# Attention in bursts of three on borrowed MLP banks: 49 bursts in place of 73 in a fused attention and MLP kernel

## Chip, cores, metric

One core of a Trainium2 chip. The metric is the time of one execution on the device in microseconds (us).

## The reference

```python
# q, k, v: (8, 12, 448, 64);  w_in: (768, 2048);  w_out: (2048, 768);  alpha: (2048,)
scores = matmul(q, k.T) / sqrt(64)
attn_out = matmul(maximum(scores, 0) ** 2 / 448, v)
x = attn_out.transpose(0, 2, 1, 3).reshape(3584, 768)
h = x @ w_in
out = (maximum(h, 0) + alpha * minimum(h, 0)) @ w_out
```

## The kernel before

The engines are named as in the profile: PE is the tensor engine (PEld its weight loads), ACT is ScalarE, DVE is VectorE, POOL is GpSimd, SP issues DMAs. Matmul results go to PSUM, of which the kernel uses eight banks (two pairs and four); a bank gets its next tile only when ACT or DVE have read the last one.

The heads of a batch are taken four at a time: a "quad", three per batch, 24 in all. A quad has seven chunks of scores, each 4 matmuls on 64*64 quarters of the array, then A@V, 28 such matmuls. Each batch has an MLP in two stages: "in" (16 tiles `hps` of 6 matmuls, 128*128) and "out" (tiles `ops` of 16 matmuls in two half steps; 12 half steps in even batches, 16 in odd ones). The attention of batch b+1 is put in bursts between the MLP steps of batch b.

```python
sc_ps = pool("scps", 2, **PSUM)      # two pairs of banks: a chunk of scores, or an A@V
mm_ps = pool("mmps", 4, **PSUM)      # four banks for hps and ops
neg_pool = pool("neg", 3)

def scores(n, j, relu="act", space=sc_ps):
    ...                                          # 4 matmuls into two banks
    if relu == "both":                           # one bank by ACT, one by DVE
        nc.scalar.activation(rl[:, 0], half[0][:, :S], ACTF.Relu)
        nc.vector.tensor_scalar(rl[:, 1], half[1][:, :S], 0.0, None, ALU.max)
    ...
    else:
        nc.scalar.activation(rl, ps[:, :, :S], ACTF.Relu)

def squares(...):  nc.vector.tensor_tensor(a, rl, rl, ALU.mult)      # for each chunk

def ffn1(b, ff, ...):                            # one hps tile
    ...                                          # 6 matmuls
    nc.scalar.activation(neg, ps, ACTF.Relu, scale=-1.0)
    nc.vector.scalar_tensor_tensor(gT[...], neg, beta_sb[...], ps, ALU.mult, ALU.add)

def burst(n, i):                                 # four per quad
    if i == 0:                                   # chunk 0, then A@V of the quad before
        scores(n, 0); squares(); attnv(n - 1)
    else:                                        # chunks 2i-1 and 2i
        for j in (2 * i - 1, 2 * i):
            scores(n, j, ...); squares()
    if i == 0: load(n + 2)                       # each cut here: n below the number of quads
    if i == 1: transpose(n + 1, "k"); transpose(n + 1, "q")     # by DMA
    if i == 2: to_bf16(n + 2, w, nc.gpsimd)      # casts of k, q, v on GpSimd

for b in range(2, B - 1):                        # 12 bursts over the 28 or 32 steps of a batch
    spread(steps(b, "in") + steps(b, "out"), work[12 * b - 11:12 * b + 1])
```

## Time and profile before

| | before |
|---|---|
| time, median of the first 3 runs | 405.86 us (405.38 to 406.36) |
| span in the profile | 403.4 us |
| tensor engine (PE) busy | 390.4 us, 97% |
| attention bursts in the stream of quads 6 to 23 | 73 |

PE is busy nearly always, so the question is what it is busy with. The prediction shows the chain and a stretch of PE's timeline. Three groups of the page: line, engine, operation, output<-input, shapes and count; then total busy us and mean ns of one; then the engine's idle time before them.

```profile
L170 ACT ACTIVATE rl<-sc 128x896 bf16<-128x896 f32 x156 | 136.2, 919 | 80.0 <-PE sc L159 76.7
L181 DVE TENSOR_TENSOR at<-rl 128x896 bf16<-128x896 bf16 x167 | 115.2, 702 | 55.2 <-ACT rl L170 51.0
L236 DVE SCALAR_TENSOR_TENSOR gT<-neg,beta_sb,hps 128x448 bf16<-128x448 f32 x128 | 84.8, 676 | 31.8 <-ACT neg L235 30.7
```

Every chunk costs one ReLU on ACT and one square on DVE; every hps tile ends in one gT update on DVE, and only then is its bank free. Both engines mostly wait for someone else, and neither bounds the kernel.

### The profile page before, as it was taken

To read this page: it belongs to the slowest core of one execution; us is meant where nothing else is said; L and a number is where in the kernel's file an instruction comes from. 1 tells how busy PE (TensorE), PEld (TensorE's weight loads), DVE (VectorE), ACT (ScalarE), POOL (GpSimd) and SP (SyncE) were. 2 spreads that over 40 slices of the span, in tenths; PEclk is the share of its full clock that TensorE was granted. 3 is DMA by queue.
4 is the path that set the end of the run, shared out by engine and by line. 5 is a ranking of instruction groups with operands and counts; after the bars stand their busy time and mean duration, and the time that the engine had idled before them with its cause. 6 is when DMAs were issued, how large, how long until landed. Compare 5 with 4: busy or idle time off the path is not lost.

```text
span 403.4 us, 7848 instructions
## 1 busy us (share of the span) xinstructions
PE 390.4 (97%) x3201; PEld 196.0 (49%) x3201; DVE 241.8 (60%) x379; ACT 232.1 (58%) x330; POOL 76.1 (19%) x88
## 2 busy tenths in 40 slices
PE   7689999999999999999999999999999999999995
PEld 4334455444555445544555445544455444555562
DVE  3966766687464793488643975556834666525411
ACT  5866745787564885387643876557653577524200
POOL 6653000033033330035000350033300300000000
PEclk9999999999999999999999999999999999999999
DMA  6999996593278941586065862379054720130033
GB/s 143 196 209 204 204 249 205 121 283 78 65 197 240 288 87 45 160 248 183 0 118 178 225 186 46 85 223 312 4 79 105 205 46 2 41 78 2 1 80 78
DMA packets 64164, 55.44 MB, mean 137 GB/s; under 512 B 35696, under 2 KB 59776, under 8 KB 64128
## 3 DMA queue, kind: packets, MB, share of 16 engines
q1 hardware_dynamic: 53152, 44.98, 41.6%
q0 software_dynamic: 10976, 9.96, 15.5%
q8 instruction: 25, 0.41, 0.4%
q14 instruction: 11, 0.09, 0.1%
HBM read 45.62 MB, written 11.01 MB: 140 GB/s over the span
## 4 chain that ended last, share of the span: by engine, by line
PE 90%; DMA 8%; issue 0%; ACT 0%; DVE 0%; SPq 0%; POOL 0%; POOLq 0%
PE ops L244 37%; PE hps L228 35%; PE sc L159 10%; PE av L199 7%; DMA qe<-in_q_dram 3%; DMA w_in_sb<-in_moe_w_in_dram 2%; DMA vb<-in_v_dram 2%; DMA kraw<-in_k_dram 1%; PE tps L134 1%; ACT xT L214 0%; DVE osb L252 0%; ACT ke L335 0%; SPq L321 0%; POOL ke L103 0%; PE warm L317 0%
## 5 line engine op out<-in xcount | busy, mean ns | idle before, releaser
L170 ACT ACTIVATE rl<-sc 128x896 bf16<-128x896 f32 x156 | 136.2, 919 | 80.0 <-PE sc L159 76.7
L228 PE MATMUL hps<-xT,w_in_sb 128*128 128x448 bf16 x768 | 154.8, 353 | 1.3 <-ACT xT L208 0.5
L244 PE MATMUL ops<-w_out_sb,gT 128*128 128x384 bf16 x896 | 154.3, 327 | 0.0
L181 DVE TENSOR_TENSOR at<-rl 128x896 bf16<-128x896 bf16 x167 | 115.2, 702 | 55.2 <-ACT rl L170 51.0
L244 PEld LDWEIGHTS <-gT 128*128 128x128 bf16 x896 | 84.0, 98 | 67.0 <-issue 14.5
L228 PEld LDWEIGHTS <-w_in_sb 128*128 128x128 bf16 x768 | 71.3, 98 | 79.0 <-issue 18.2
L236 DVE SCALAR_TENSOR_TENSOR gT<-neg,beta_sb,hps 128x448 bf16<-128x448 f32 x128 | 84.8, 676 | 31.8 <-ACT neg L235 30.7
L235 ACT ACTIVATE neg<-hps 128x448 f32<-128x448 f32 x128 | 69.8, 549 | 46.0 <-PE hps L228 45.4
L252 DVE COPY osb<-ops 128x384 f32<-128x384 f32 x56 | 31.1, 555 | 58.4 <-PE ops L244 58.4
L109 POOL CAST kb<-kraw 128x896 bf16<-128x896 f32 x16 | 16.1, 1007 | 210.4 <-DMA vraw<-in_v_dram 121.8
L159 PE MATMUL sc<-qT,kT 64*64 64x448 bf16 x652 | 50.8, 364 | 3.7 <-ACT rl L170 1.6
L199 PE MATMUL av<-at,vb 64*64 64x448 bf16 x616 | 33.1, 350 | 0.0
L159 PEld LDWEIGHTS <-kT 64*64 64x64 bf16 x672 | 14.5, 104 | 37.2 <-issue 33.7
L214 ACT ACTIVATE xT<-av 128x896 bf16<-128x896 f32 x21 | 19.3, 917 | 11.3 <-PE av L199 11.3
L199 PEld LDWEIGHTS <-vb 64*64 64x64 bf16 x672 | 19.7, 107 | 11.5 <-issue 1.7
L109 POOL CAST qb<-qraw 128x896 bf16<-128x896 f32 x16 | 20.0, 1250 | 0.0
L109 POOL CAST vb<-vraw 128x896 bf16<-128x896 f32 x16 | 18.6, 1165 | 0.4 <-DMA vraw<-in_v_dram 0.3
L144 POOL DMA_DIRECT2D w_in_sb<-in_moe_w_in_dram x12 | 7.5, 636 | 4.7 <-DMA vb<-in_v_dram 1.8
L168 DVE TENSOR_SCALAR rl<-sc 128x896 bf16<-128x896 f32 x6 | 6.5, 1086 | 2.9 <-PE sc L159 2.9
L317 PE MATMUL warm<-warm_x,warm_w 128*128 128x256 bf16 x24 | 4.6, 359 | 1.1 <-DVE warm_x L311 1.1
L134 PE MATMUL tps<-ident,ke 128*64 128x128 bf16 x84 | 3.7, 222 | 1.2 <-ACT rl L165 0.6
L107 ACT COPY kT<-tps 128x896 bf16<-128x896 bf16 (+1 forms) x4 | 3.2, 798 | 2.8 <-PE tps L134 2.7
(46 smaller groups left out, 59.0 us busy)
## 6 DMA issues: line engine op xcount, KB each, us to landing
out_dram<-osb SPq DMA_DIRECT2D x56, 192.0 KB, 2.7
qraw<-in_q_dram SPq DMA_DIRECT2D x19, 448.0 KB, 4.1
kraw<-in_k_dram SPq DMA_DIRECT2D x19, 448.0 KB, 5.0
vraw<-in_v_dram SPq DMA_DIRECT2D x18, 448.0 KB, 5.7
w_out_sb<-in_moe_w_out_dram POOLq DMA_DIRECT2D x2, 1536.0 KB, 20.2
w_in_sb<-in_moe_w_in_dram POOLq DMA_DIRECT2D x8, 192.0 KB, 8.4
w_in_sb<-in_moe_w_in_dram POOLq DMA_DIRECT2D x4, 384.0 KB, 9.9
vb<-in_v_dram POOLq DMA_DIRECT2D x6, 224.0 KB, 9.8
```

The costliest lines, as they stand in the source:

```text
L109: eng.tensor_copy(o, i)
L134: nc.tensor.transpose(ps[64 * s:64 * s + 64, j], t[:, s, j], ident)
L159: nc.tensor.matmul(half[r][64 * c:64 * c + 64, :S], kT[n][64 * r:64 * r + 64, j, c, :], qT[n][64 * r:64 * r + 64, :, c, :], start=True, st ...
L170: nc.scalar.activation(rl, ps[:, :, :S], ACTF.Relu)
L181: nc.vector.tensor_tensor(a, rl, rl, ALU.mult)
L199: nc.tensor.matmul(half[r][64 * s:64 * s + 64, :S], vb[n][64 * r:64 * r + 64, s, j, :], a[64 * r:64 * r + 64, s], start=(j == 0), stop=(j ...
L214: nc.scalar.activation(xT[b][:, g], ps[:, :, :S], ACTF.Copy, scale=out_scale)
L228: nc.tensor.matmul(ps, w_in_sb[:, km // 2, km % 2, bass.ts(ff, 128)], xT[b][:, km // 2, km % 2, :], start=(km == 0), stop=(km == KM - 1))
L235: nc.scalar.activation(neg, ps, ACTF.Relu, scale=-1.0)
L236: nc.vector.scalar_tensor_tensor(gT[b // 2][:, ff, (b % 2) * S:(b % 2) * S + S], neg, beta_sb[:, ff:ff + 1], ps, ALU.mult, ALU.add)
L244: nc.tensor.matmul(ps, gT[sb][:, ff, bass.ts(c, 128)], w_out_sb[:, ff, bass.ts(hf, 384)], start=(ff == 0), stop=(ff == KF - 1))
L252: nc.vector.tensor_copy(o[:, bass.ts(hf, 384)], ps)
```

## The change

Its intent: fewer bursts. Three units (a unit is a chunk or an A@V) go in one burst. There are only two pairs of score banks, so the first chunk of a burst borrows two of the four MLP banks. In the "in" stage ACT takes both its halves, in the "out" stage ACT and DVE one each. Most bursts go to the "out" stage. The DMA transposes move to the burst that holds chunk 0, and the A@V of a quad comes one chunk later.

```diff
+        elif relu == "act2":
+            for r in range(2):
+                nc.scalar.activation(rl[:, r], half[r][:, :S], ACTF.Relu)
...
-    for b in range(2, B - 1):
-        spread(steps(b, "in") + steps(b, "out"), work[12 * b - 11:12 * b + 1])
+    stream = []
+    for n in range(2 * NG, NQ):
+        for j in range(NJ):
+            stream.append((n, j))
+            if j == 1 and n > 2 * NG:
+                stream.append((n - 1, "av"))
+    stream.append((NQ - 1, "av"))
...      # parts: the first of 2 units, then of 3
+            units_ = sorted(units, key=lambda u: u[1] == "av")
+            for i, (n, j) in enumerate(units_):
+                if j == "av":
+                    attnv(n)
+                elif i == 0 and len(units_) == 3:
+                    scores(n, j, "act2" if phase == "in" else "both", mm_ps)
+                else:
+                    scores(n, j)
+            squares()
...      # chunk 0: load(n + 2), transpose(n + 1); chunk 4: to_bf16(n + 2)
+    for b in range(1, B - 1):
+        n_in, n_out = ((2, 6) if b % 2 else (3, 5))
...
+        spread(mlp[3:] if b == 1 else mlp, [group(x, "in") for x in parts[count:count + n_in]], 0.95)
+        spread(steps(b, "out"), [group(x, "out") for x in parts[count:count + n_out]], 0.92)
```

More of the change, by code (lines that the diff above doesn't have):

```diff
@@ L281, in burst @@
                 squares()
-        if n < n_pe:
-            return
-        if i == 0 and n + 2 < NQ:
-            load(n + 2)
-        if i == 1 and n + 1 < NQ:
-            transpose(n + 1, "k")
-            transpose(n + 1, "q")
-        if i == 2 and n + 2 < NQ:
-            for w in "kqv":
-                to_bf16(n + 2, w, nc.gpsimd)
     def spread(seq, bursts, share=0.92):
@@ L412, with group, f @@
         ffn1(1, ff, range(4, KM))
-    work = [(n, i) for n in range(2 * NG, NQ) for i in range(4)] + [(NQ, 0)]
-    mlp = steps(1, "in")
-    spread(mlp[3:] + steps(1, "out"), work[:13])
-    for b in range(2, B - 1):
-        spread(steps(b, "in") + steps(b, "out"), work[12 * b - 11:12 * b + 1])
+    stream = []
[5 more added lines that the diff above has]
+    stream.append((NQ - 1, "av"))
+    parts, todo_u = [], list(stream)
+    while todo_u:
+        m = 2 if not parts else 3
+        parts.append(todo_u[:m])
+        del todo_u[:m]
+    def group(units, phase):
+        def f():
+            units_ = sorted(units, key=lambda u: u[1] == "av")
[7 more added lines that the diff above has]
+            squares()
+            for n, j in units_:
+                if j == 0:
+                    if n + 2 < NQ:
+                        load(n + 2)
+                    if n + 1 < NQ:
+                        transpose(n + 1, "k")
+                        transpose(n + 1, "q")
+                if j == 4 and n + 2 < NQ:
+                    for w in "kqv":
+                        to_bf16(n + 2, w, nc.gpsimd)
+        return f
+    count = 0
+    for b in range(1, B - 1):
+        n_in, n_out = ((2, 6) if b % 2 else (3, 5))
+        if b == 1:
+            n_in += 1
+        if b == B - 2:
+            n_out = len(parts) - count - n_in
+        mlp = steps(b, "in")
+        spread(mlp[3:] if b == 1 else mlp, [group(x, "in") for x in parts[count:count + n_in]], 0.95)
+        count += n_in
+        spread(steps(b, "out"), [group(x, "out") for x in parts[count:count + n_out]], 0.92)
+        count += n_out
     for _, fn in steps(B - 1, "in") + steps(B - 1, "out"):
```

## The prediction

> **What bounds the kernel now.** I read the page first: the shares of the engines, then the chain that ended last, then the waits from 127 to 355 us (batches 2 to 6 of the stream that the change rewrites), then the timeline of the tensor engine at a burst.
>
> ```profile
> PE 390.4 (97%) x3201; PEld 196.0 (49%) x3201; DVE 241.8 (60%) x379; ACT 232.1 (58%) x330; POOL 76.1 (19%) x88
> PE 90%; DMA 8%; issue 0%; ACT 0%; DVE 0%; SPq 0%; POOL 0%; POOLq 0%
> ```
>
> PE is busy for 97% of the span and makes up 90% of the chain; the 8% of DMA is the start, before 35 us, which the change doesn't touch. In the view of the waits from 127 to 355 us no row has PE as the one that waits: everybody waits for PE. So only PE time counts, and the question is which PE time isn't arithmetic. The timeline of PE (start, duration, count last) shows it:
>
> ```profile
> 175.10 0.57 PE L159 MATMUL sc<-qT,kT 64*64 64x448 bf16 x8
> 175.60 3.58 PE L228 MATMUL hps<-xT,w_in_sb 128*128 128x448 bf16 x18
> 179.11 0.57 PE L159 MATMUL sc<-qT,kT 64*64 64x448 bf16 x8
> 179.62 2.44 PE L228 MATMUL hps<-xT,w_in_sb 128*128 128x448 bf16 x12
> 181.99 0.38 PE L159 MATMUL sc<-qT,kT 64*64 64x448 bf16 x4
> 182.20 1.49 PE L199 MATMUL av<-at,vb 64*64 64x448 bf16 x28
> ```
>
> Starts are measured; ends are modelled, so I use starts only. Record by record, hps matmuls start 189 ns apart and ops matmuls 163. Four 64*64 matmuls start within about 10 ns of each other and the next four some 190 later, so a quartet is one step of 189 ns. Take the time from the last MLP matmul before a burst to the second after it, less two MLP steps: 609 ns for 8 scores, 1744 for 4 scores and 28 av, 1554 for the 28 av alone. Less 2, 8 and 7 steps of 189 that is 231, 232 and 231 ns. So **every burst pays a fixed 0.231 us**, whatever its length, beside hps and ops alike (94 ns entering, about 24 inside the first quartet, 92 leaving, the rest in the first MLP steps).
>
> A second, smaller loss, in the timeline of all engines:
>
> ```profile
> 253.16 0.57 PE L159 MATMUL sc<-qT,kT 64*64 64x448 bf16 x8
> 253.60 1.73 ACT L170 ACTIVATE rl<-sc 128x896 bf16<-128x896 f32 x2 [1.48 <-PE sc L159]
> 253.67 1.47 PE L244 MATMUL ops<-w_out_sb,gT 128*128 128x384 bf16 x8
> 255.07 0.69 PE L159 MATMUL sc<-qT,kT 64*64 64x448 bf16 x8
> ```
>
> Where only half an ops tile (8 matmuls) lies between two bursts, the second quartet starts late, because the ReLU at 253.60 holds the second score bank pair until 255.33: 722 ns instead of 608, four times in the stream.
>
> **What the Trainium skill says.** "TensorEngine Tiling (Array Packing)", Key Properties: changing the tiling mode drains the tensor engine; the 94 and 92 ns at each end of a burst agree, and the trace adds the size of it. "TensorE: Matmul & The Clock Gate", Back-to-back issue gap: N/2.4 + 2.5 ns for an isolated warm matmul, so 189 for 448 columns and 162.5 for 384, and less (131 for 512) in a sustained stream. The trace has 189 and 163 in its streams: the first formula holds here, and MLP steps have nothing left to give. "SBUF — State Buffer", Who interferes with whom: a VectorE instruction with two SBUF inputs contends with a GpSimd one that reads SBUF. The trace agrees: squares (L181) take 0.625 us, and up to 1.37 us where a POOL cast runs. "PSUM — Partial Sum Buffer" says in its rules to evacuate promptly; the ReLU wait above is such a case.
>
> **The change part by part.**
>
> *Removed.* Before: 18 quads in four bursts plus a last one, 73 bursts (I counted 73 runs of 64*64 matmuls after 79 us). After: 18 x 7 chunks and 18 A@V are 144 units; a first burst of 2, 47 of 3, a last of 1 make 49. 24 fewer, 24 x 0.231 = 5.54 us, all on PE and so on the chain. The matmuls stay the same in number and size.
>
> *Removed, by spacing.* In the second MLP stage ("out") bursts now lie at least two ops half-steps (2.6 us) apart: before steps 0, 3, 5, 8, 10, 13 of 16 for odd batches, 0, 3, 5, 7, 9 of 12 for even ones. The four waits of 0.114 go: 0.46 us.
>
> *Added, "out" stage.* Three chunks at once: the first on two MLP banks, half by ACT (0.55 us, as L235), half by DVE (616 by L166), two on the score banks. From the burst's first score matmul, in us: the quartets end at 0.37, 0.56, 0.75; ACT begins 0.06 later, back to back about 0.44 for a half and 0.81 for a whole, so the ReLUs end near 0.98, 1.8, 2.6; the squares follow 0.03 later each, the third ends at 3.26. The next burst comes at 0.69 + 16 x 0.163 + 0.09 = 3.4 at the earliest. Its score banks have been free since 2.6, and the borrowed MLP banks since 1.05. A whole odd "out" stage gives DVE 15 squares, 6 halves and 8 copies (0.555), 17.5 us, in about 29 us of PE. Nothing new on the path.
>
> *Added, "in" stage.* Both halves go to ACT, before the whole chunks, so ReLUs end near 3.1 and the first gT update (DVE, 0.68) comes at 3.8 to 4.4 behind three squares. The fifth hps tile after the burst, first to need a bank that the MLP gives back, starts at 0.69 + 4 x 1.13 = 5.2. Slack 0.8 us without casts. Casts (k, q, v: 1.0, 1.25, 1.17 us) fall into this stage, as now (POOL is busy there and idle in the "out" stretches I looked at), and can lengthen two or three squares by 0.7 each. There are 15 such bursts; if one in four loses the slack and some 0.15 to 0.2 us more, that is about 0.6 us. This is the softest figure.
>
> *Moved.* The load of quad n+2 and the DMA transposes of n+1 go to the burst with chunk 0. Transposes land in 2.6 to 6.7 us and are needed a whole quad later, at the closest 11 us (even "out" stage); loads take 4 to 5.5. Hidden. A@V of a batch's last quad stands with three steps (3.9 us) left, and its eviction to xT takes 0.92, ending about 2.9 after the burst's start, when the MLP still has some 2.9 to do. Hidden. The at tiles at most meet a wait of DVE on the A@V of the same burst.
>
> Sum: 405.86 - 5.54 - 0.46 + 0.6 = 400.5 us.
>
> **The rivals.**
>
> *A wait for MLP banks in the "out" stage.* The ops tile under way at a burst is copied only behind the burst's three squares, from 3.2 to 3.75. If the four MLP buffers went in strict rotation, the next burst at 3.4 would get just that bank and wait 0.4 us. It happens where a burst of three score chunks in mid-tile is followed two steps later by one that borrows banks: twice in batches 2 and 4, once each in 1, 3, 5 and 6, 8 x 0.4 = 3.2 us, giving 403.1 to 403.7. Against it: the compiled kernel before doesn't take these four banks in rotation where borrowed and MLP tiles mix early on; it takes the one freed first, and here the two ReLU banks are free two microseconds sooner. I lean against, but it sets the upper side.
>
> *DVE becomes the bound of the "in" stage.* DVE and ACT are already busiest there (14.0 and 14.5 us of 18.6 in one stretch, against 12.3 and 12.5 of 25 in an "out" one), and casts fall on bursts of three squares, not two. If all 15 bursts lost 0.3 us: 4.5 us, about 404. Against it: the change puts fewer units there (6 or 9 where an odd batch had 12), so the average load drops.
>
> *The transposes come late.* Loads go ahead of them in one queue. If both were slow, up to 10 us stand against 11: then a stall of a microsecond or two per batch, 403 to 406. It has slack nearly everywhere, and in even batches the queue reaches the load long before.
>
> *The drain isn't fixed* but grows with the burst: 12 scores might cost more than 231 + 3 x 189. The equal remainders at 2, 7 and 8 quartets speak against it.
>
> **Range and chances.** With no new wait at all it is 399.9, and only the run-to-run spread (405.38 to 406.36) can take it below that; every doubt but that one adds time, so the range is lopsided: 399.2 to 402.9, which holds the first rival only in part. Faster by over 2% needs under 397.7, some 8 us, when all the removable loss I find is 6.0: chance 0.02. Slower by over 2% needs over 414, two rivals at once and more: 0.01. Within 2%: 0.97.
>
> **What would show it.** In the changed trace: 49 runs of 64*64 matmuls after 79 us, each with 231 ns beyond 189 per quartet (798 for 12 scores, by the same measure); no PE row in the waits of the stream for gT, osb or sch, or rows summing to under 1 us; the chain still about 90% PE; squares of 1.3 us only beside casts. The prediction is wrong if bursts keep 189 per quartet but PE rows with DVE as releaser add up to microseconds, if the quartets themselves spread, or if PE waits for a transpose at chunk 0.

## The result and the profile after

Ratios here are the mean time of one kernel's fast runs over that of the other's of the same rounds, so not quite the ratio of the medians quoted.

| | before | after |
|---|---|---|
| time, median | 406.11 us (405.38 to 407.26, 4 runs) | 401.06 us (400.39 to 401.54, 4 runs) |
| ratio | | 0.9872 (95% interval 0.9848 to 0.9895) |
| span in the profile | 403.4 us | 399.3 us |
| bursts in the stream | 73 | 49 |
| stream, in the profile | 322.18 us | 316.73 us |

The gain is 1.3%, clear of the noise but under the 2% from which the record calls a change faster, so its verdict there is "same".

"Stream" is the time from the first matmul of the A@V of quad 5, at about 76 us, to the start of the kernel's last matmul. Everything before it is the same in both kernels.

The page's first line and its chain, after:

```profile
PE 387.3 (97%) x3201; PEld 200.8 (50%) x3201; DVE 258.1 (65%) x411; ACT 221.0 (55%) x345; POOL 72.8 (18%) x88
PE 92%; DVE 2%; DMA 2%; ACT 1%; issue 1%; POOL 0%; ACTq 0%
```

The same 3201 matmuls, 97% busy still, 92% of the chain. DVE has come into the chain with 2%; about half of that lies in the start, before 34 us, and most of the rest is one burst at 311.94, where the chain passes through three squares slowed by casts (3.47 us). PE's timeline across the change from "in" to "out" of batch 2:

```profile
148.83 0.38 PE L159 MATMUL sch<-qT,kT 64*64 64x448 bf16 x4
149.04 0.55 PE L159 MATMUL sc<-qT,kT 64*64 64x448 bf16 x8
149.52 4.07 PE L247 MATMUL ops<-w_out_sb,gT 128*128 128x384 bf16 x24
153.52 0.38 PE L159 MATMUL sch<-qT,kT 64*64 64x448 bf16 x4
153.74 0.55 PE L159 MATMUL sc<-qT,kT 64*64 64x448 bf16 x8
154.22 2.77 PE L247 MATMUL ops<-w_out_sb,gT 128*128 128x384 bf16 x16
156.92 0.38 PE L159 MATMUL sch<-qT,kT 64*64 64x448 bf16 x4
```

`sch` is the chunk on borrowed banks. From 153.52 to the next MLP start at 154.22 it is 0.70 us for 12 scores, where 8 took 0.50 (175.10 to 175.60 before): a third quartet costs its 0.19 and nothing else. Measured as in the prediction, all 49 bursts of the stream have 229 to 233 ns beyond 189 per quartet; no score matmul waits for a bank. The waits from 80 to 352 us have no row in which PE waits for DVE (their one PE row, 0.2 us for ACT at 79.92, is the wait that the kernel before has at 78.47). But they count idle time from the modelled end of a matmul, 0.35 us after its start, so a matmul that is late by up to 0.3 us leaves no row here. By start times, the hps matmuls of the "in" stage come 44, 45, 166 and 299 ns late at four bursts of the stream, 0.55 us together. The sum closes: 322.18 - 24 x 0.231 - 4 x 0.114 + 0.55 = 316.73.

The two profiles' starts differ by 1.45 us (the stream begins at 75.93 and at 77.38) though the instructions are the same; the profile after had 6.8 us of half TensorE clock in there. So the spans differ by less than the streams.

### The profile page after: what moved, and what is told of

The parts are those of the page before. It is cut to its first block, busy times and chain, and to the rows that moved or that the text cites. A ratio compares the mean times of both kernels' runs of the same rounds, so it can differ in the third digit from the quotient of the medians.

```text
span 399.3 us, 7923 instructions
## 1 busy us (share of the span) xinstructions
PE 387.3 (97%) x3201; PEld 200.8 (50%) x3201; DVE 258.1 (65%) x411; ACT 221.0 (55%) x345; POOL 72.8 (18%) x88
## 4 chain that ended last, share of the span: by engine, by line
PE 92%; DVE 2%; DMA 2%; ACT 1%; issue 1%; POOL 0%; ACTq 0%
PE ops L247 38%; PE hps L231 35%; PE av L202 7%; PE sc L159 6%; PE sch L159 4%; DMA qe<-in_q_dram 2%; DVE at L184 1%; PE tps L134 1%; DMA qraw<-in_q_dram 1%; PE avh L202 1%; ACT rl L173 0%; DVE gT L239 0%; ACT xT L211 0%; ACT xT L217 0%; POOL ke L103 0%
## 5 line engine op out<-in xcount | busy, mean ns | idle before, releaser
L231 PE MATMUL hps<-xT,w_in_sb 128*128 128x448 bf16 x768 | 151.2, 353 | 1.4 <-ACT xT L211 0.5
L184 DVE TENSOR_TENSOR at<-rl 128x896 bf16<-128x896 bf16 x167 | 111.1, 685 | 19.0 <-ACT rl L173 8.8
L231 PEld LDWEIGHTS <-w_in_sb 128*128 128x128 bf16 x768 | 73.1, 98 | 75.7 <-issue 10.2
L173 ACT ACTIVATE rl<-sc 128x896 bf16<-128x896 f32 x109 | 95.8, 927 | 7.7 <-PE sc L159 5.3
L165 ACT ACTIVATE rl<-sch 128x448 bf16<-128x448 f32 x37 | 20.1, 544 | 56.4 <-PE sch L159 56.4
L159 PE MATMUL sc<-qT,kT 64*64 64x448 bf16 x464 | 36.4, 362 | 2.7 <-ACT rl L173 2.2
L166 DVE TENSOR_SCALAR rl<-sch 128x448 bf16<-128x448 f32 x37 | 23.0, 620 | 14.1 <-PE sch L159 14.1
L169 ACT ACTIVATE rl<-sch 128x448 bf16<-128x448 f32 x30 | 14.6, 544 | 16.9 <-PE sch L159 16.9
L159 PE MATMUL sch<-qT,kT 64*64 64x448 bf16 x208 | 20.3, 380 | 0.0
L109 POOL CAST qb<-qraw 128x896 bf16<-128x896 f32 x16 | 18.4, 1151 | 0.0
L109 POOL CAST vb<-vraw 128x896 bf16<-128x896 f32 x16 | 16.8, 1053 | 1.4 <-DMA vraw<-in_v_dram 0.8
```

Of the source, the lines that this page charges most:

```text
L109: eng.tensor_copy(o, i)
L159: nc.tensor.matmul(half[r][64 * c:64 * c + 64, :S], kT[n][64 * r:64 * r + 64, j, c, :], qT[n][64 * r:64 * r + 64, :, c, :], start=True, st ...
L231: nc.tensor.matmul(ps, w_in_sb[:, km // 2, km % 2, bass.ts(ff, 128)], xT[b][:, km // 2, km % 2, :], start=(km == 0), stop=(km == KM - 1))
```

## The experiments

Each is an edit of the changed kernel. The first four ran on one chip, the other four on another chip, each with its own runs of the kernel before.

### The changed kernel again

No edit.

> The changed kernel once more, as the yardstick for the other runs of this chip. Between two profiles the stream is 5.45 us shorter (24 bursts x 0.231 = 5.53, four ReLU waits 0.46 gone, 0.55 of new waits in the first MLP stage); the rest of the difference lies in the start, where one profile had a stretch of half clock. Expected ratio to before 0.986 to 0.988.

401.23 us (399.46 to 401.9, 5 runs), before 405.86, ratio 0.9895 (0.9878 to 0.9911). The stream was 316.46 us, with 0.28 us of late hps matmuls at two bursts. The ratio came out 0.0015 above the expected band, and the runs spread over 2.4 us where the kernel before spreads over 0.7.

### Bursts of two in the new order

```diff
-    parts, todo_u = [], list(stream)
+    parts, todo_u = [], list(stream[:-1])
...
-        m = 2 if not parts else 3
-        parts.append(todo_u[:m])
-        del todo_u[:m]
+        parts.append(todo_u[:2])
+        del todo_u[:2]
+    parts.append(stream[-1:])
...      # 12 parts per batch (13 in batch 1) over "in" and "out" together, the last A@V alone
```

> The new order of units, the new places of loads, casts and transposes, but bursts of two (73 bursts, no borrowed MLP banks), spread evenly as in the kernel before. Theory (the gain is the number of bursts): within 0.5 us of before, ratio 0.999 to 1.002, every burst again 0.231 beyond 0.189 per quartet. Rival (order, moved loads or spacing give the gain): ratio near the changed kernel's 0.987.

405.95 us, before 405.86, ratio 1.0007 (0.9992 to 1.0022). 73 bursts, each 231 ns beyond its quartets except three with 114 ns more. So the new order, the later A@V and the moved transposes are worth nothing by themselves, within this interval. The rival falls.

### Bursts of one

```diff
-    parts, todo_u = [], list(stream)
-    while todo_u:
-        m = 2 if not parts else 3
...
+    parts = [[u] for u in stream]
...      # 24 parts per batch (26 in batch 1), spread as in the pairs
```

> Bursts of one: 144 bursts of one chunk or one A@V, otherwise the changed kernel's stream. Theory (a fixed 0.231 us per burst): 95 more bursts than the changed kernel cost 21.9 us, so about 423 us, plus what waits come of DVE being asked for a square per step (up to 2 us). Rival (the cost goes with the work in a burst, or drains overlap when bursts are short): under 412 us.

420.3 us, ratio to before 1.036 (1.0345 to 1.0376). I had expected 423. The trace has 141 bursts, not 144: at three places two parts fell on the same step and became one.

```profile
151.18 0.38 PE L159 MATMUL sc<-qT,kT 64*64 64x448 bf16 x4
151.49 1.31 PE L231 MATMUL hps<-xT,w_in_sb 128*128 128x448 bf16 x6
152.73 0.38 PE L159 MATMUL sc<-qT,kT 64*64 64x448 bf16 x4
153.05 1.31 PE L231 MATMUL hps<-xT,w_in_sb 128*128 128x448 bf16 x6
154.19 1.46 PE L247 MATMUL ops<-w_out_sb,gT 128*128 128x384 bf16 x8
```

One period is 152.73 - 151.18 = 1.55 us; six hps matmuls and one quartet are 7 x 0.189 = 1.32; the rest is the 0.23 again. From hps to ops matmuls, both 128*128, nothing is lost: 154.19 - 153.05 = 1.14 us is six hps steps. So it is not any change of operands that costs 0.23, but the visit to 64*64. The stream is 337.42 us, 20.69 more than in the first profile after; that profile's 0.55 of late hps matmuls is not there, so 92 bursts cost 21.24 us, 0.231 each. The cost per burst is thus the same for one quartet as for nine. The medians differ by only 19.1 us from the changed kernel's: its unprofiled runs were slower than its profiled one (399.46), which the next experiments explain in part.

### Strict rotation of the MLP banks

```diff
-    mm_ps = pool("mmps", 4, **PSUM)
+    class Rotation:
...      # self.pools: four pools of one bank each
+        def tile(self, *args, **kw):
+            self.n += 1
+            return self.pools[self.n % 4].tile(*args, **kw)
+    mm_ps = Rotation()
```

> The changed kernel with its four MLP banks handed out in strict rotation, where the compiled program otherwise takes the one freed first. If my first rival's working was right about its cost, the tensor engine waits for the bank of the ops tile in mid-flight, about 0.4 us, at eight bursts: 3.2 us more, 404 to 404.5 us, with waits of scores on the copy of ops. If banks don't matter at all: 401. Rotation may also change the start by a microsecond either way, so the trace of the stream decides.

404.75 us (402.73 to 405.56), before 405.86, ratio 0.9967. Eight bursts start late by 359 to 363 ns, one or two in each batch as the first rival had counted them. PE's row in the waits, and the timeline of one (the idle time in the last bracket is again counted from a modelled end):

```profile
PE sch L167 <- DVE osb L263: 2.3, 8, 0.3
```

```profile
153.17 2.77 PE L255 MATMUL ops<-w_out_sb,gT 128*128 128x384 bf16 x16
153.33 1.72 ACT L181 ACTIVATE rl<-sc 128x896 bf16<-128x896 f32 x2
...
155.09 0.62 DVE L192 TENSOR_TENSOR at<-rl 128x896 bf16<-128x896 bf16 x1 [0.18 <-ACT rl L181]
155.63 0.55 DVE L263 COPY osb<-ops 128x384 f32<-128x384 f32 x1
...
156.23 0.38 PE L167 MATMUL sch<-qT,kT 64*64 64x448 bf16 x4 [0.29 <-DVE osb L263]
```

The ops tile was complete by 154.7 (half of its 16 matmuls come after 153.17), but its copy stands behind the third square in DVE's queue and ends at 156.18; the next burst, due at 155.87, gets just that bank. Eight times 0.36 is 2.9 us of the stream; late hps matmuls were 2.04 us more, so the sum 316.18 + 2.89 + 2.04 gives the 321.1 measured (316.18 is the stream without any wait: 316.73 - 0.55; the memset run below, which has none, took 316.19). The 2.9 us are rotation's; the late hps matmuls may not be, as the changed kernel has up to 2.17 us of them in another profile (below). By the medians of these rounds rotation takes back 3.5 of the 4.6 us gained, and whether the change pays depends on which bank a tile is given.

### The changed kernel a third time, and casts that don't read

This pair is about the late hps matmuls of the "in" stage, which no two profiles had at the same bursts. First the control:

> The changed kernel a third time, for this chip and these rounds. Ratio to before 0.986 to 0.990. In the trace no burst above 0.235 us, and between 0.2 and 1.2 us of waits of hps matmuls in the first MLP stage, at other bursts than in the two profiles before (0.55 and 0.28 us), since they depend on when loads land and casts start. If that is so, the runs spread more widely than those of before (before: 0.7 us; this: over 1.5 us).

401.47 us (400.95 to 402.29), before 405.82, ratio 0.99 (0.9886 to 0.9914). The stream was 318.34 us, with 2.17 us of late hps matmuls at six bursts: nearly twice what I had allowed (1.2). The spread was not over 1.5 us this time, and the kernel before had 1.8 in its nine runs, so the spread tells nothing. This time the waits (from 80 to 352 us) have a row for it, and the last of the six is seen in the timeline of all engines:

```profile
PE hps L231 <- DVE gT L239: 1.4, 3, 0.5
```

```profile
312.39 0.38 PE L159 MATMUL sch<-qT,kT 64*64 64x448 bf16 x4
...
313.08 4.71 PE L231 MATMUL hps<-xT,w_in_sb 128*128 128x448 bf16 x24
...
313.72 0.93 POOL L109 CAST kb<-kraw 128x896 bf16<-128x896 f32 x1 [10.77 <-DMA kraw<-in_k_dram]
313.82 3.85 DVE L184 TENSOR_TENSOR at<-rl 128x896 bf16<-128x896 bf16 x3 [0.76 <-ACT rl L169]
...
314.59 1.33 POOL L109 CAST qb<-qraw 128x896 bf16<-128x896 f32 x1
...
315.86 1.32 POOL L109 CAST vb<-vraw 128x896 bf16<-128x896 f32 x1
...
317.59 1.26 DVE L239 SCALAR_TENSOR_TENSOR gT<-neg,beta_sb,hps 128x448 bf16<-128x448 f32 x2
318.31 0.54 PE L231 MATMUL hps<-xT,w_in_sb 128*128 128x448 bf16 x2 [0.52 <-DVE gT L239]
```

The k load lands and three casts run from 313.72 to 317.18. Three squares take 3.85 us instead of 1.9, so the first gT update comes at 317.59. The fifth hps tile, due 24 steps of 189 ns after 313.08, at 317.62, starts at 318.31: it waits for the bank that the update frees. Now the same without casts that read:

```diff
+    def fill(o, i):                       # wrong result on purpose
+        nc.gpsimd.memset(o, 0.03)
+        nc.gpsimd.tensor_copy(o[:, 0, 0, 0:1], i[:, 0, 0, 0:1])
...      # in to_bf16: fill() in place of the cast, where it is on GpSimd
```

> WRONG RESULT ON PURPOSE: the GpSimd casts of the stream only fill their tile and copy one column, so GpSimd hardly reads SBUF any more. Theory (the waits of the first MLP stage come from casts that slow the squares): no square above 0.75 us in the stream, no wait of an hps matmul on gT, 0.3 to 1 us faster than the changed kernel in the same rounds, spread of the runs under 1 us. Rival (three chunks at once are too much for ACT and DVE even without casts): the waits stay, same time.

400.53 us (400.2 to 401.0), ratio to before 0.9879 (0.9864 to 0.9894), against the control's 401.47 and 0.99 of the same rounds; wrong result, as meant. The groups of the squares and of one of the three fills:

```profile
L194 DVE TENSOR_TENSOR at<-rl 128x896 bf16<-128x896 bf16 x167 | 101.6, 624 | 21.4 <-ACT rl L183 11.1 <-ACT rl L179 5.7
L112 POOL MEMSET kb<- 128x896 bf16 x16 | 13.5, 845 | 48.1 <-DMA kT<-kb 47.1 <-ACT neg L248 1.0
```

The squares' mean falls to 624 ns (702 before, 685 in the first profile after), with none over 627 in the stream, though GpSimd still spends 0.85 us on each tile. No hps matmul is late, and the stream is 316.19 us, 2.15 less than in the control. (The control's profiled run was its slowest, this one's its fastest; the medians differ by 0.94 us.) So it is the casts that make the tensor engine wait, and the three-chunk burst only where a cast meets it. That it is their reading and not some other trait is likely, not shown: the fill also is another operation, and shorter (0.85 us against 0.93 to 1.33).

### One square at a time in the "in" stage

```diff
             fn()
+            if todo:
+                squares(keep=len(todo) - 1)        # after each MLP step, one
...      # in group():
-            squares()
+            if phase == "in":
+                squares(keep=len(todo) - 1)
+            else:
+                squares()
```

> Right result. In the first MLP stage only the first square follows the burst, the others come one by one after the next hps tiles, so that a gT update waits behind at most one slow square. Theory: the waits of hps in that stage vanish though the casts stay: 0.3 to 1 us faster than the changed kernel, small spread. If the casts cause the waits in another way than through the order on DVE, they stay.

401.7 us, ratio 0.9906 (0.9893 to 0.9919): no better than the control. No hps matmul was late, as expected, but four bursts of the "in" stage were, by 0.12 to 0.91 us, 2.36 us in all:

```profile
141.16 0.38 PE L159 MATMUL sch<-qT,kT 64*64 64x448 bf16 x2
...
141.35 1.85 DVE L239 SCALAR_TENSOR_TENSOR gT<-neg,beta_sb,hps 128x448 bf16<-128x448 f32 x3
...
142.07 0.38 PE L159 MATMUL sch<-qT,kT 64*64 64x448 bf16 x2 [0.53 <-DVE gT L239]
```

The first half of the borrowed chunk starts at once, the second waits 0.91 us for a bank whose gT update is still queued on DVE. The slow squares now stand between later updates, and the wait has moved from the fifth hps tile to the next burst's second bank. Why that bank and not another was given to it I did not settle. This idea failed.

### Bursts of five

If PE's cost is the number of bursts and the banks of the first chunks are free again after the 1.3 us of an A@V, a burst can be longer than its banks.

```diff
+        m = 2 if not parts else 5 if any(u[1] == "av" for u in todo_u[:3]) else 3
...      # order in a burst of five: chunk, chunk on MLP banks, A@V, chunk, chunk on MLP banks
+                if len(units) == 5:
+                    squares(keep=1)
...      # n_in, n_out = (1, 5) in odd batches, (2, 4) in even ones; rl of 4 and at of 12 buffers
```

> Right result. The A@V bursts hold five units: a chunk on the score banks, a chunk on MLP banks, A@V, and two more chunks on banks that the first two have freed meanwhile; 38 bursts instead of 49. Theory: 11 x 0.231 = 2.5 us less, and fewer bursts in the first MLP stage: 398 to 399 us, ratio to before 0.981 to 0.983, 1420 ns expected for 0 but 231 beyond 9+... that is 231 ns beyond 189 per quartet (11 quartets) in each burst of five. Rival (the banks of the first chunks are not free when the fourth and fifth come, or DVE falls behind): quartets inside the burst start late and bursts show 300 ns or more; then no gain.

397.27 us (396.43 to 397.83), right result, ratio to before 0.9793 (0.9778 to 0.9807): 4.2 us faster than the control of the same rounds. A burst of five:

```profile
107.88 0.38 PE L159 MATMUL sc<-qT,kT 64*64 64x448 bf16 x4
108.09 0.36 PE L159 MATMUL sch<-qT,kT 64*64 64x448 bf16 x4
108.28 1.49 PE L202 MATMUL av<-at,vb 64*64 64x448 bf16 x28
109.60 0.36 PE L159 MATMUL sc<-qT,kT 64*64 64x448 bf16 x4
109.79 0.36 PE L159 MATMUL sch<-qT,kT 64*64 64x448 bf16 x4
110.08 2.12 PE L247 MATMUL ops<-w_out_sb,gT 128*128 128x384 bf16 x12
```

Every start follows the last by 0.19 per quartet: the fourth and fifth unit do not wait. All 38 bursts have 229 to 233 ns beyond their quartets. (The "1420 ns" in the expectation is a slip of mine; the same sentence mends it.) The stream is 314.09 us: 316.18 - 11 x 0.231 + 0.45 of late hps matmuls at one burst. It is 4.25 us shorter than the control's: 2.54 are the 11 bursts, 1.72 that the control waited 2.17 and this one 0.45 in the "in" stage, which has fewer bursts now. The second part changes from run to run, and the profiled run of the control was its slowest. This version beats both kernels: all its runs are under all of theirs. Against the kernel before it gains 2.1%; whether that is over 2%, the interval leaves unclear.

## Why the prediction was right

**Right: a fixed 0.231 us per burst, 24 of them.** Seen at 1, 2, 3, 7, 8, 9 and 11 quartets and at 38, 49, 73 and 141 bursts. Undoing the burst length (pairs, and with it the borrowed banks and the spacing) undid the whole gain.

**Right: the four ReLU waits go.** No burst after is beyond 233 ns. Three of them are back in the pairs.

**Right: nothing new in the "out" stage.** In three profiles no burst or ops step of it waits. The first rival was sized at 0.4 us in eight places; made to happen, it was 0.36 in eight places. It stayed away because the compiled program doesn't hand out the banks in strict rotation. That it gives the bank freed first, as the prediction says, fits the missing waits, but no trace here names the banks.

**Right in kind, loose in size: waits in the "in" stage, put at 0.6 us.** Three profiles show 0.55, 0.28 and 2.17. The mechanism is the one named (casts, slow squares, a late gT update, the fifth hps tile), shown by replacing the casts. The slack of 0.8 us without casts holds: in the memset run the first gT update ends 4.3 to 4.4 us after the start of a burst of three chunks, and the fifth hps tile starts at 5.2 to 5.3. That the first profile came so near, with four of the fifteen bursts as guessed, is luck: the second had two, the third six, and the third's PE row of 1.4 us is over the 1 us that the prediction had set as a sign. (Three of the fifteen hold an A@V and only two squares; none of these was late.) The waits depend on when a load lands and its casts start, so one number for them was too neat.

**Open: the start.** The median lies 0.56 us above the prediction. In the profiled run (401.45) the "in" waits were 0.55, as forecast, and the stream gained 5.45 us, but it began 1.45 us later, with 6.8 us of half clock before it; the prediction took the start as unchanged. The memset kernel's median is 5.3 us under that of before, not the 6.0 of the streams; in the two profiles the missing 0.7 is just the later start (76.64 against 75.93, with 3.4 us of half clock before it). What the unprofiled runs did, no trace shows.

**Right: transposes, loads and xT stay hidden.** (The prediction calls the loads moved, too; in the kernel before they already stood with chunk 0.) In no profile has PE's stream a row of waits with a DMA as its releaser.

## What to carry to other kernels

Where PE switches between tilings of the array, count the switches: price one from matmul start times, then make the bursts longer and not more frequent. Buffers bound the length only while the first ones are in use, so a long unit in mid-burst (here A@V) can win them back. A buffer borrowed from another stage is safe only as long as its release doesn't stand in an engine's queue behind the new work, so look at which buffer the program gives out and what its releaser does first.

## What the Trainium skill lacked or had wrong

- "TensorEngine Tiling (Array Packing)", Key Properties: says that a mode change drains the engine, without a size. Here a visit to 64*64 mode and back costs 0.231 us (about 94 ns entering, 24 in the first quartet, 92 leaving, the rest after), the same for 4 to 44 matmuls and beside 384 and 448 columns.
- "TensorE: Matmul & The Clock Gate", Back-to-back issue gap: the lower sustained figure (131 ns at 512 columns) is not seen, though no run here has 512 columns; the longest streams, 96 and 128 matmuls at the end of the kernel, run at 189 ns for 448 columns and 163 for 384, as its formula for an isolated gap has it (189.2 and 162.5).
- "SBUF — State Buffer", Who interferes with whom: its rule on VectorE instructions with two SBUF inputs held in both directions (squares of 625 ns took up to 1407 beside casts, and at most 627 beside memsets), but the page has no figure for such a pair, and the cast pays too (0.93 us alone, 1.33 beside squares).
